# First W1 chunk loaded ahead of the values, first keys ahead of the first queries, and a new set of ranks, in a sparse-attention and feed-forward kernel

## The chip, the cores and the metric

The kernel runs on one core of a Trainium2 chip. The metric is device time in microseconds of one execution; the number to predict is the median of such executions. The core has a matrix engine (TensorE, PE in the profile; its weight loads are PEld), a vector engine (VectorE, DVE), a scalar engine (ScalarE, ACT), GpSimd (POOL) and a queue engine (SyncE, SP) that here only issues DMAs. Each engine works through its own list of instructions in order and waits at semaphores for the others.

## What is computed

```python
def reference(q, k, v, sampled_blocks, g_ln, w_ch1, w_ch2):      # B=4, H=8, S=768, D=64
    scores = q @ k^T / sqrt(64)
    # 24 blocks of 32: neighbours, the first and last block, and 3 sampled blocks per row
    scores = where(mask, scores, -1e9)
    attn = softmax(scores) ; x = (attn @ v) as [4, 768, 512]
    xn = (x - mean(x)) / sqrt(var(x) + 1e-6) * g_ln
    return x + relu(xn @ w_ch1) @ w_ch2                             # 512 -> 2048 -> 512
```

The two weight matrices come as 64-bit floats (4 bytes of each element's 8 cannot be used directly), so the kernel rebuilds 32-bit numbers from the bits on the chip and splits each into a high and a low 16-bit half.

## The kernel before, in words

**Tiling.** The 4 x 768 queries are cut into 12 units of 256 (`units`). A unit has four segments (`segs`, 48 in all), one for each pair of heads, and a segment has four slots: a slot is one head and 128 queries against all 768 keys. For a segment, TensorE forms scores in two groups (`scores`, L602, 12 matmuls a group, the two heads of 128 queries; the first segment uses 32-bit operands). VectorE adds the mask and takes the row maximum (`masked_max`, L611), ScalarE exponentiates (`exponent`, L625). In the first nine segments (`EARLY`) TensorE then transposes the probabilities (L640), ScalarE copies them out of the accumulators (L647) and TensorE multiplies by the values (L728); the later segments transpose by DMA. After four segments a unit is normalised (`layer_norm`: L809, L827, L838, L863, L877) and goes through the two products of the feed-forward part (`ffn`, both at L313, operands `w1h`, `w1l`, then `w2h`, `w2l`).

**Weights.** W1 is handled in 8 chunks (1 MB each), W2 in 16 (512 KB each). `loads_w` issues the load of a chunk (L508, L518), VectorE shifts and masks the bits in two or three operations (L529, L533, then L537, or L542 with an addition on GpSimd at L547), ScalarE scales and forms the high half (L565, L571, L573; a few by DMA at L583), and the low half is a subtraction on VectorE or GpSimd (L579, L577). The keys and queries are split in a like manner (L363, L370, L395, L400). Which engine does which step of which chunk stands in the tables `PORC`, `HIDMA`, `LOWDVE`, `KDVE`, `QDVE`, `CASTQ`, `XDVE`.

**Order.** Nothing is ordered by hand. Each step is a task of a `Plan` with an engine, a cost, what it comes after, and a rank. `Plan.run` goes through planned time and, on each engine, takes among the tasks that can start soonest the one of lowest rank; the instructions are emitted in that order. The rank of a step of attention is about its slot's number; the loads and splits of keys, values and queries are placed by `KAT`, `VAT`, `QAT`, the chunks of W1 and W2 by the tables `W1AT` and `W2AT`, with the load itself at `rank - LEAD`. Where the plan sees TensorE idle it puts in matmuls on constants into a free accumulator (`filler`, L305), which compute nothing that is used.

**Loads.** All loads named here are issued by SP, in the plan's order. The program gives the DMAs of the SP and ACT queues eight completion semaphores in turn, so from the ninth on each issue first waits for the load eight places before it.

In the kernel before, the first chunk's load is a task that comes after the first keys and the first queries:

```python
        if i == 0:
            lw.after += [kt[0, 0].raw, qt[0].raw]
```

Of the kernel before, what the change touches and what calls it, by code (L numbers as in the profile page):

```python
# [176 lines left out]
def sparse_attention_moe(  # L177
# [14 lines left out]
    B, NPAIR, NCH, _, CH = qs.shape  # L192
# [13 lines left out]
    UPS = H * TS  # L206

    EARLY = 9
    EARLYLN = 1
    EASY, EASE = 34, (232, 2529, 1055)  # L210
    PORC = ((2, 0), (2, 7), (1, 1), (2, 13), (2, 10), (1, 4), (2, 1), (1, 0))
    XACT = 4
    XDVE = 0
    RAWS_S = 1
    SPLITAT = 13.44
    VDVE = 1
    KDVE, QDVE = 12, 5
    HIDMA = ((1, 1), (1, 6), (2, 5), (2, 3), (2, 12), (2, 6), (2, 2), (2, 4))
    LEAD = -4.15
    POOLQ = ()  # L220
    WIDEAT = 16
    HIGHAT, LOWAT = -3.61, 0.01
    EVAC, EXPO = -23.3, 2.93
    PLAIN = 'full'
    LOWDVE = ((2, 2), (1, 1), (2, 11), (1, 7), (2, 4), (2, 6), (2, 3), (1, 0), (2, 9), (2, 13), (1, 6), (1, 2))
    AVHOLD = 4
    KEEP = 90000.0
    CASTK, CASTQ = 16, 5
    MASKAT = 11.99
    KAT, VAT, QAT = 4.32, 10.55, 11.84  # L230
    AVAT = -18.16
    W1AT = (5.59, 9.73, 14.79, 15.09, 18.96, 21.75, 22.98, 26.73)
    W2AT = (4.96, 6.46, 7.35, 7.59, 7.79, 8.12, 8.15, 8.19, 8.29, 8.43, 8.78, 8.9, 10.5, 10.66, 10.72, 13.23)

# [20 lines left out]
    plan = Plan()  # L255
# [226 lines left out]
    def loads_w(kind, i, before, w1done, low_tail):  # L482

        o = SimpleNamespace()
        own = (kind, i)
# [64 lines left out]
        if kind == 2 and i >= 10:  # L550
            after += tuple(low_tail)
        ld = plan.add(*queue_of(qw)[1:], load, after if kind == 1 or i >= 10 else after + tuple(
            w1done if not low_tail and i > 1 else ()), rank - LEAD, 2000,
            load=2900 * size, take=take, order="w")
        o.load = ld
# [438 lines left out]
    for b in range(B):  # L994
        for pr in range(NPAIR):
            order.append(((UPS * NCH * b) + 4 * pr - (8 if b else KAT), 0, b, pr))
            order.append(((UPS * NCH * b) + 4 * pr + VAT, 2, b, pr))
# [157 lines left out]
```

## Time and profile before

| | |
|---|---|
| time, median of 3 runs | 792.12 us (791.73 to 793.36) |
| span of the profiled execution (first to last instruction) | 790.0 us |
| PE busy in that span | 778.1 us, 98% |
| DVE, ACT, POOL busy | 621.5, 509.4, 105.2 us |

The profile's own time is its span; 2.1 us of the median lie outside it (792.12 less 790.0). In the profile a busy PE is a PE with at least one matmul under way; matmuls are pipelined, so busy time overlaps and a short wait can hide inside it.

### The profile page before, as it was taken

What the parts mean: (1) busy time and instruction counts of PE and PEld (TensorE: products, weight loads), DVE (VectorE), ACT (ScalarE), POOL (GpSimd) and SP (SyncE); (2) the same over time, 40 slices, a digit from 0 to 9 for tenths busy, and PEclk for the clock granted to TensorE, in tenths of its full rate; (3) what the DMA queues carried; (4) which work ended last, traced back from release to release, by engine and by line L of the source; (5) the groups of instructions that cost most, each with busy time, mean ns of one, the idle gap of its engine ahead of it and who ended that gap; (6) DMA issues with size and microseconds to landing.
All of it is one profiled execution on the core that took longest, in us unless ns stands there. A gap on an engine that the chain in (4) does not pass through costs nothing.

```text
span 790.0 us, 18464 instructions
## 1 busy us (share of the span) xinstructions
PE 778.1 (98%) x7336; PEld 600.0 (76%) x7336; DVE 621.5 (79%) x1225; ACT 509.4 (64%) x948; POOL 105.2 (13%) x117
## 2 busy tenths in 40 slices
PE   8999999999999999999999999999999999999998
PEld 5655677778777777777777777777777777788887
DVE  6989999988988788989878878888877878854220
ACT  6888876687666667777766766667656657652110
POOL 0444332200101000001011012021000100000000
PEclk9999999999999999999999999999999999999999
DMA  9553545978977688998785787887766656561000
GB/s 324 181 147 109 161 135 153 231 161 164 165 134 129 139 128 162 169 192 157 144 135 124 132 163 132 172 166 156 137 131 112 140 118 110 121 122 25 21 1 27
DMA packets 285638, 109.27 MB, mean 138 GB/s; under 512 B 253808, under 2 KB 277360, under 8 KB 285552
## 3 DMA queue, kind: packets, MB, share of 16 engines
q1 hardware_dynamic: 278544, 104.91, 61.1%
q0 software_dynamic: 6720, 3.08, 3.5%
q8 instruction: 57, 0.93, 0.5%
q14 instruction: 29, 0.24, 0.1%
q10 hardware_dynamic: 288, 0.10, 0.1%
HBM read 42.97 MB, written 6.29 MB: 62 GB/s over the span
## 4 chain that ended last, share of the span: by engine, by line
PE 89%; DVE 6%; ACT 2%; DMA 1%; issue 1%; SPq 1%; POOL 0%; ACTq 0%
PE bank L313 65%; PE ps L602 11%; PE pa L732 7%; PE pa L737 3%; PE pa L728 1%; DVE p L611 1%; DMA w1r<-w 1%; PE bank L640 1%; DVE w2h L533 1%; ACT pt L647 1%; DVE w2h L529 0%; DVE allow L328 0%; DVE w2h L537 0%; ACT p L625 0%; POOL w2h L547 0%
## 5 line engine op out<-in xcount | busy, mean ns | idle before, releaser
L313 PE MATMUL bank<-hh,w2h 128*128 128x256 f16 x768 | 204.5, 273 | 0.0
L313 PE MATMUL bank<-hh,w2l 128*128 128x256 f16 x768 | 204.1, 273 | 0.0
L313 PE MATMUL bank<-hl,w2h 128*128 128x256 f16 x768 | 204.1, 273 | 0.0
L611 DVE CUSTOM_DVE_ANT_1 p<-ps,allow 128x768 f32<-128x768 f32 x184 | 170.1, 951 | 24.0 <-PE ps L602 23.8
L625 ACT ACTIVATE p<-p,st 128x768 f32<-128x768 f32 x184 | 170.5, 928 | 15.7 <-DVE st L611 15.5
L313 PEld LDWEIGHTS <-w2h 128*128 128x128 f16 x1536 | 147.4, 98 | 25.8 <-issue 8.9
L313 PEld LDWEIGHTS <-w1h 128*128 128x128 f16 x1536 | 148.7, 98 | 23.6 <-issue 6.7
L313 PE MATMUL bank<-xh,w1h 128*128 128x256 f16 x768 | 115.4, 273 | 1.4 <-ACT pt L647 1.4
L313 PE MATMUL bank<-xh,w1l 128*128 128x256 f16 x768 | 115.4, 273 | 0.0
L313 PE MATMUL bank<-xl,w1h 128*128 128x256 f16 x768 | 115.3, 273 | 0.0
L916 DVE SCALAR_TENSOR_TENSOR hl<-bank,hh 128x512 f16<-128x512 f32 x96 | 66.2, 689 | 48.5 <-ACT hh L910 47.7
L910 ACT ACTIVATE hh<-bank 128x512 f16<-128x512 f32 x96 | 57.0, 594 | 65.4 <-PE bank L313 64.7
L688 ACT ACTIVATE ph<-p,st 128x768 f16<-128x768 f32 x92 | 83.5, 927 | 19.6 <-issue 8.2
L692 DVE SCALAR_TENSOR_TENSOR pl<-p,st,ph 128x768 f16<-128x768 f32 x92 | 94.3, 1042 | 1.2 <-DMA pt<-pl 1.0
L313 PEld LDWEIGHTS <-w1l 128*128 128x128 f16 x768 | 73.3, 98 | 13.7 <-issue 5.5
L313 PEld LDWEIGHTS <-w2l 128*128 128x128 f16 x768 | 75.0, 98 | 8.9 <-issue 0.2
L732 PE MATMUL pa<-pt,vh 128*64 128x512 f16 x468 | 79.2, 383 | 0.0
L688 ACT ACTIVATE raw<-p,st 128x768 f16<-128x768 f32 x64 | 57.9, 928 | 25.6 <-issue 14.7
L397 POOL DMA_DIRECT2D qh<-q x43 | 24.6, 571 | 333.7 <-PE ps L602 299.7
L692 DVE SCALAR_TENSOR_TENSOR raw<-p,st,raw 128x768 f16<-128x768 f32 x64 | 67.0, 1062 | 0.0
L602 PE MATMUL ps<-kh,qh 64*128 64x512 f16 (+1 forms) x376 | 64.9, 328 | 0.6 <-DVE st L611 0.5
L737 PE MATMUL pa<-pt,vl 128*64 128x256 f16 x468 | 64.6, 273 | 0.0
(125 smaller groups left out, 986.7 us busy)
## 6 DMA issues: line engine op xcount, KB each, us to landing
qr<-q SPq DMA_DIRECT2D x48, 128.0 KB, 3.0
raw<-k SPq DMA_DIRECT2D x16, 384.0 KB, 3.9
vr<-v SPq DMA_DIRECT2D x32, 192.0 KB, 2.9
out<-ot SPq DMA_DIRECT2D x48, 128.0 KB, 1.9
raw<-w SPq DMA_DIRECT2D x11, 512.0 KB, 3.8
w2l<-w SPq DMA_DIRECT2D x4, 1024.0 KB, 8.0
qh<-q POOLq DMA_DIRECT2D x43, 64.0 KB, 3.0
w1r<-w SPq DMA_DIRECT2D x2, 1024.0 KB, 8.3
```

The lines of the kernel that those rows point to most:

```text
L313: nc.tensor.matmul(dst, w, x, start=start, stop=stop, skip_group_check=True)
L397: o.high = plan.add("POOL", 560, lambda: nc.gpsimd.dma_start(o.qh, qs[u.b, pr, u.c]), (o.raw,), rank, 2300, load=600, order="q")
L533: nc.vector.scalar_tensor_tensor(out=o.wf, in0=o.raw[:, :, 1], scalar=-0x40000000, in1=o.wf, op0=ALU.bitwise_and, op1=ALU.bitwise_or)
L602: nc.tensor.matmul(s.ps[:, lo:hi], x[rows, s.qs], y[rows, lo:hi], start=n == 0, stop=n == len(terms) - 1)
L611: nc.vector.tensor_tensor_reduce(out=s.p.rearrange(blk, k=BLK), in0=s.ps[:, 0:S].rearrange(blk, k=BLK), in1=bias, scale=-0.125, scalar=3.0 ...
L625: nc.scalar.activation(s.p, s.p, AF.Exp, bias=s.st[:, j : j + 1], scale=-1.0, accum_out=total)
L688: nc.scalar.activation(s.ph, s.p, AF.Copy, scale=s.r)
L692: nc.vector.scalar_tensor_tensor(out=s.pl, in0=s.p, scalar=s.r, in1=s.ph, op0=ALU.mult, op1=ALU.subtract)
L732: nc.tensor.matmul(seg.pa[half[hh], 0 : 2 * CH], vo.vh[:, hh, t, :], pts[keys[hh]][:, t].rearrange("p i n -> p (i n)"), start=t == 0, stop ...
L737: nc.tensor.matmul(seg.pa[half[hh], 0:CH], vo.vl[:, hh, t, :], pts[keys[hh]][:, t, 0, :], start=False, stop=t == KT - 1, skip_group_check= ...
L910: nc.scalar.activation(u.hh[:, f : f + 2, :].rearrange("p f n -> p (f n)"), bank[plan.where("bank", own)], AF.Relu)
L916: nc.vector.scalar_tensor_tensor(out=u.hl[:, f : f + 2, :].rearrange("p f n -> p (f n)"), in0=bank[plan.where("bank", own)], scalar=0.0, i ...
```

## The change

The load of W1's first chunk no longer comes after the first keys and queries, and gets a rank of its own (`W1LEAD`); the first keys get one, too (`KFIRST`). All other numbers of placement are new, some steps change engines, and 61 tasks get a number added to their rank by a new table (`NUDGE`).

```diff
-    EASY, EASE = 34, (232, 2529, 1055)
-    PORC = ((2, 0), (2, 7), (1, 1), (2, 13), (2, 10), (1, 4), (2, 1), (1, 0))
+    EASY, EASE = 36, (232, 2529, 1055)
+    PORC = ((1, 1), (1, 5), (2, 0), (2, 1), (2, 3), (2, 5), (2, 7), (2, 10))
-    XDVE = 0
+    XDVE = 2
-    KDVE, QDVE = 12, 5
+    KDVE, QDVE = 8, 10
+    W1LEAD = -1.21
+    KFIRST = -12.57
-    LOWDVE = ((2, 2), (1, 1), (2, 11), (1, 7), (2, 4), (2, 6), (2, 3), (1, 0), (2, 9), (2, 13), (1, 6), (1, 2))
+    LOWDVE = ((1, 1), (1, 6), (1, 7), (2, 0), (2, 3), (2, 4), (2, 5), (2, 6), (2, 7), (2, 9), (2, 10), (2, 13), (2, 15))
-    CASTK, CASTQ = 16, 5
+    CASTK, CASTQ = 16, 7
-    MASKAT = 11.99
-    KAT, VAT, QAT = 4.32, 10.55, 11.84
+    MASKAT = 32.06
+    KAT, VAT, QAT = 8.91, 8.01, 3.36
+    NUDGE = {
+        1: 88.6, 31: -99.5, 41: 65.7, 46: -97.0, 273: 113.4, 282: 0.9, 288: -223.4, 296: 18.5,
...
         ld = plan.add(*queue_of(qw)[1:], load, after if kind == 1 or i >= 10 else after + tuple(
-            w1done if not low_tail and i > 1 else ()), rank - LEAD, 2000,
-            load=2900 * size, take=take, order="w")
+            w1done if not low_tail and i > 1 else ()), W1LEAD if own == (1, 0) else rank - LEAD,
+            2000, load=2900 * size, take=take, order="w")
...
-            order.append(((UPS * NCH * b) + 4 * pr - (8 if b else KAT), 0, b, pr))
+            order.append((KFIRST if (b, pr) == (0, 0) else (UPS * NCH * b) + 4 * pr - (8 if b else KAT), 0, b, pr))
...
-        if i == 0:
-            lw.after += [kt[0, 0].raw, qt[0].raw]
-            for x in lw.after[-2:]:
-                x.next.append(lw)
-                lw.left += 1
...
+    for n, by in NUDGE.items():
+        plan.tasks[n].rank += by
     plan.run()
```

What it does to the queues is seen at three places. Line numbers of the changed kernel are 13 higher there. First, the start of SP's queue; `raw` are keys, `qr` queries, `vh` and `vl` the first values, `w1r0`, `w1r1` and the first `w2l` the stages of W1's chunks 0, 1 and 2. Before:

```order
L388 DMA qr0_131<-q 128x256
L388 DMA qr1_133<-q 128x256
L360 DMA raw0_115<-k 128x768
L388 DMA qr2_139<-q 128x256
L360 DMA raw1_116<-k 128x768
L1015 DMA g_sb_113<-g 128x4x1
L470 DMA vh0_149<-v 128x384
L470 DMA vl0_150<-v 128x384
L470 DMA vh1_155<-v 128x384
L508 DMA w1r0_189<-w1 128x4x512
L508 DMA w1r1_193<-w1 128x4x512
```

and in the changed kernel:

```order
L373 DMA raw0_115<-k 128x768
L373 DMA raw1_116<-k 128x768
L401 DMA qr0_137<-q 128x256
L521 DMA w1r0_139<-w1 128x4x512
L401 DMA qr1_141<-q 128x256
L521 DMA w1r1_144<-w1 128x4x512
L521 DMA w2l_130<-w1 128x4x512
L401 DMA qr2_158<-q 128x256
L483 DMA vh0_189<-v 128x384
L483 DMA vl0_190<-v 128x384
```

Chunk 0 moves from the tenth issue to the fourth, chunks 1 and 2 come ahead of the first values as well, and the first queries move from first to third.

Second, VectorE's queue from the first pair of maxima on (each maximum is a row of `p` at L611 or L624, with a row of its accumulator `st` behind it). Before:

```order
L611 ISA p0_121,st0_201<-ps0_183,allow_109 128x768
L611 ISA st0_201 128x1
L363 TENSOR_TENSOR kl1_143<-raw1_116,kh1_142 128x768
L611 ISA p1_122,st0_201<-ps1_184,allow_109 128x768
L611 ISA st0_201 128x1
L529 TENSOR_SCALAR w2h_129<-w1r0_189 128x1024
L611 ISA p2_123,st2_255<-ps2_240,allow_109 128x768
L611 ISA st2_255 128x1
L611 ISA p3_124,st2_255<-ps3_241,allow_109 128x768
L611 ISA st2_255 128x1
L533 SCALAR_TENSOR_TENSOR w2h_129<-w1r0_189,w2h_129 128x1024
```

and in the changed kernel:

```order
L624 ISA p1_122,st0_197<-ps1_184,allow_109 128x768
L624 ISA st0_197 128x1
L542 TENSOR_SCALAR w2h_129<-w1r0_139 128x1024
L413 TENSOR_TENSOR ql0_117<-qr1_141,qh1_142 128x256
L546 SCALAR_TENSOR_TENSOR w2h_129<-w1r0_139,w2h_129 128x1024
L624 ISA p2_123,st2_238<-ps2_222,allow_109 128x768
L624 ISA st2_238 128x1
L550 SCALAR_TENSOR_TENSOR w2h_129<-w1r0_139,w2h_129 128x1024
L660 COPY pt0_0_244<-bank2_100 128x2x128
L624 ISA p3_124,st2_238<-ps3_223,allow_109 128x768
```

The three steps on chunk 0 now stand between the second and the fourth maximum, and a copy of transposed probabilities, ScalarE's work before, is among them.

Third, VectorE's queue where the second part of the mask is built (`allow`, L325 to L330 before). Before, it stands ahead of the ninth and tenth maximum:

```order
L542 TENSOR_SCALAR w1r1_193<-w1r1_193 128x1024
L325 TENSOR_TENSOR w1h_127<-allow_109,samp_i_110 128x288
L328 TENSOR_TENSOR allow_109<-allow_109,w1h_127 128x96 x3
L330 TENSOR_SCALAR allow_109<-allow_109 128x96
L760 TENSOR_TENSOR xT0_372<-pa0_373,xT0_372 128x256
L611 ISA p2_123,st8_435<-ps8_416,allow_109 128x768
```

and in the changed kernel behind them:

```order
L624 ISA p3_124,st8_448<-ps9_428,allow_109 128x768
L624 ISA st8_448 128x1
L413 TENSOR_TENSOR ql2_119<-qr3_251,qh3_252 128x256
L338 TENSOR_TENSOR w1h_127<-allow_109,samp_i_110 128x288
L341 TENSOR_TENSOR allow_109<-allow_109,w1h_127 128x96 x3
L343 TENSOR_SCALAR allow_109<-allow_109 128x96
L624 ISA ph_125,st10_494<-ps10_473,allow_109 128x768
```

The mask's second part moves behind the fifth pair of maxima, and steps on chunks 0 to 2 of W1 take its place.

## Rows read from the trace of the kernel before

**Rows 1.** Windows: stretch, its length, busy us by engine (count), clock, DMA share, GB/s

```profile
0.00:20.00 20.00, 17.40 (x124) 11.88 (x125) 13.13 (x31) 12.48 (x24) 1.27 (x7) 1.00 0.92 325
20.00:60.00 40.00, 36.57 (x321) 24.03 (x321) 37.36 (x65) 33.76 (x73) 17.73 (x13) 1.00 0.56 168
60.00:100.00 40.00, 37.59 (x320) 25.24 (x320) 38.87 (x71) 35.34 (x80) 13.86 (x13) 1.00 0.43 135
100.00:700.00 600.00, 600.00 (x5779) 463.06 (x5774) 505.57 (x1013) 410.29 (x742) 72.29 (x86) 1.00 0.74 147
700.00:790.00 90.00, 86.55 (x801) 75.75 (x799) 26.61 (x49) 17.54 (x33) 0.00 (x0) 1.00 0.14 30
```

**Rows 2.** Waits of PE: who waited for whom, us in total, times, longest

```profile
PE bank L640 <- ACT pt L647: 3.4, 6, 1.1
PE bank L313 <- ACT pt L647: 1.4, 1, 1.4
```

**Rows 3.** Groups by form: shapes, count, busy us, mean ns, idle before

```profile
L305 PE MATMUL bank<-ones,ones_h 128*128 128x256 f16 x84 | 11.9, 298 | 1.2 <-DVE eps L280 1.2
```

**Rows 4.** Chain that ended last: start us, us, what, in the head

```profile
44.01 1.08 PE ps L602 x12
45.68 2.74 PE pa L728 x24
...
74.61 1.08 PE ps L602 x12
...
102.89 7.86 PE bank L313 x72
110.75 1.08 PE ps L602 x12
```

**Rows 5.** Timeline, first 13 us: start, us, engine, line, instruction, idle before it

```profile
0.74 0.89 SPq L388 DMA_DIRECT2D qr<-q  x2
...
1.69 0.43 SPq L360 DMA_DIRECT2D raw<-k  x1
...
5.13 1.28 SPq L508 DMA_DIRECT2D w1r<-w  x2
...
6.04 0.83 ACT L370 CAST kh<-raw 128x768 f16<-128x768 f32 x1 [1.78 <-DMA raw<-k]
...
6.15 1.56 PE L602 MATMUL ps<-raw,qr 64*128 64x512 f32 x8 [1.20 <-DMA raw<-k]
...
9.86 0.95 DVE L611 CUSTOM_DVE_ANT_1 p<-ps,allow 128x768 f32<-128x768 f32 x1
...
12.52 0.70 DVE L529 TENSOR_SCALAR w2h<-w1r 128x1024 int32<-128x1024 int32 x1 [1.71 <-DMA w1r<-w]
```

**Rows 6.** DMA rate in GB/s, one number per us from 0 to 40

```profile
GB/s 0 24 252 239 360 341 163 311 389 404 412 397 395 386 396 412 411 413 414 388 404 395 405 401 407 413 331 84 116 166 23 253 24 54 0 8 0 0 0 0
```

**Rows 7.** Timeline of DVE from 17 us: the next row's start ends a step

```profile
17.77 0.95 DVE L611 CUSTOM_DVE_ANT_1 pl<-ps,allow 128x768 f32<-128x768 f32 x1
...
18.65 0.69 DVE L542 TENSOR_SCALAR w1r<-w1r 128x1024 int32<-128x1024 int32 x1
19.25 1.22 DVE L533 SCALAR_TENSOR_TENSOR w2h<-w1r,w2h 128x1024 int32<-128x1024 int32 x1
20.39 0.95 DVE L611 CUSTOM_DVE_ANT_1 p<-ps,allow 128x768 f32<-128x768 f32 x1
...
24.11 0.44 DVE L325 TENSOR_TENSOR w1h<-allow,samp_i 128x288 f32<-128x288 f32 x1
24.58 2.93 DVE L328 TENSOR_TENSOR allow<-allow,w1h 128x96 f32<-128x96 f32 x3
```

**Rows 8.** Timeline of all engines: PE transposes, then POOL and DVE side by side

```profile
16.09 1.77 PE L640 MATMUL bank<-ident,p 128*128 128x128 f32 x12
...
55.85 4.24 POOL L577 TENSOR_TENSOR w1l<-w2h,w1h 128x1024 f16<-128x1024 f32 x2
...
58.41 1.71 DVE L1063 TENSOR_SCALAR nm<-nm 128x4 f32<-128x4 f32 x1 [0.91 <-ACT p L625]
```

More of the change, by code (lines that the diff above doesn't have):

```diff
@@ L209, in sparse_attention_moe @@
     EARLYLN = 1
-    EASY, EASE = 34, (232, 2529, 1055)
-    PORC = ((2, 0), (2, 7), (1, 1), (2, 13), (2, 10), (1, 4), (2, 1), (1, 0))
+    EASY, EASE = 36, (232, 2529, 1055)
+    PORC = ((1, 1), (1, 5), (2, 0), (2, 1), (2, 3), (2, 5), (2, 7), (2, 10))
     XACT = 4
-    XDVE = 0
+    XDVE = 2
     RAWS_S = 1
-    SPLITAT = 13.44
+    SPLITAT = 0.67
     VDVE = 1
-    KDVE, QDVE = 12, 5
-    HIDMA = ((1, 1), (1, 6), (2, 5), (2, 3), (2, 12), (2, 6), (2, 2), (2, 4))
-    LEAD = -4.15
+    KDVE, QDVE = 8, 10
+    HIDMA = ((1, 1), (1, 2), (1, 5), (2, 4), (2, 7), (2, 9), (2, 12), (2, 15))
+    LEAD = -1.99
+    W1LEAD = -1.21
+    KFIRST = -12.57
     POOLQ = ()
-    WIDEAT = 16
-    HIGHAT, LOWAT = -3.61, 0.01
-    EVAC, EXPO = -23.3, 2.93
+    WIDEAT = 23
+    HIGHAT, LOWAT = 2.9, -5.81
+    EVAC, EXPO = -22.76, 12.61
     PLAIN = 'full'
-    LOWDVE = ((2, 2), (1, 1), (2, 11), (1, 7), (2, 4), (2, 6), (2, 3), (1, 0), (2, 9), (2, 13), (1, 6), (1, 2))
+    LOWDVE = ((1, 1), (1, 6), (1, 7), (2, 0), (2, 3), (2, 4), (2, 5), (2, 6), (2, 7), (2, 9), (2, 10), (2, 13), (2, 15))
     AVHOLD = 4
     KEEP = 90000.0
-    CASTK, CASTQ = 16, 5
-    MASKAT = 11.99
-    KAT, VAT, QAT = 4.32, 10.55, 11.84
-    AVAT = -18.16
-    W1AT = (5.59, 9.73, 14.79, 15.09, 18.96, 21.75, 22.98, 26.73)
-    W2AT = (4.96, 6.46, 7.35, 7.59, 7.79, 8.12, 8.15, 8.19, 8.29, 8.43, 8.78, 8.9, 10.5, 10.66, 10.72, 13.23)
+    CASTK, CASTQ = 16, 7
+    MASKAT = 32.06
+    KAT, VAT, QAT = 8.91, 8.01, 3.36
+    AVAT = -22.91
+    W1AT = (-18.23, 1.52, 4.62, 6.71, 17.65, 23.09, 29.38, 31.74)
+    W2AT = (-59.17, -56.65, -41.56, -38.84, -31.54, -30.19, -30.13, -27.57, -25.65, -24.42, -22.28, -20.76, -12.67, -11.13, -6.19, -3.13)
+    NUDGE = {
[9 rows of a table added]
+    }
     const = ctx.enter_context(tc.tile_pool(name="const", bufs=1))
```

8 rows, old and new, of the table NUDGE are left out of this document.

## The prediction

> **What bounds the kernel now.** I read the windows first. From 100 to 700 us the matrix engine is busy all the time, and after 700 us it misses only the last few us, in which results are stored [rows 1]. The change takes away no matmul but filler, and after the first unit the same work follows on PE in a similar order, so those 690 us go on as they are. Only the first 100 us have room: PE is busy 91.6 of them (17.40, 36.57 and 37.59), while VectorE is busy 37.36 of 40 and 38.87 of 40 us, and ScalarE 33.76 and 35.34 [rows 1]. So the head is bound by VectorE, with ScalarE close behind. PE's seen waits there are mostly for ScalarE's copies of transposed probabilities [rows 2]; besides, 84 filler matmuls are run [rows 3].
>
> To add up what the head loses, filler included, I take PE's useful work up to a landmark from the times at which the next row starts: a score group 1.08 us, a transpose 0.136 (12 in 1.77 less the tail), an early value group 2.64 up to its successor, a feed-forward matmul 0.109 (72 in 7.86) [rows 4, 8]; for the rest I estimate 1.45 us for a 32-bit score group, 0.54 for a spread and 0.48 for a mean's matmul. **Lost time** is a landmark's time less the useful work ahead of it:
>
> - ninth score group: 44.0 - 27.3 = 16.7 us;
> - fourteenth: 74.6 - 53.0 = 21.6 us;
> - nineteenth: 110.75 - 87.9 = 22.9 us [rows 4], and from there PE loses nothing more.
>
> The changed kernel's time is 792.12 us plus the change of that 22.9. Its 790.0 us span and the 2.1 us around it move alike.
>
> **The change part by part. The first loads.** Before, queries are issued at 0.74 and the first keys at 1.69 us, chunk 0 of W1 at 5.13 [rows 5]. Keys reach ScalarE at 6.04 and the chunk reaches VectorE at 12.52, which ends a wait of 1.71 us [rows 5]. The rates [rows 6] sum to the bytes issued up to and with the keys (0.66 MB plus part of 0.1 MB of mask) at 4.6 us and up to and with the chunk (2.92 MB) at 11.1: in both, data is used 1.4 us after its bytes are through. In the new order the keys have 0.45 MB, the first queries 1.02 MB and the chunk 2.07 MB up to their end. By the same rates that is 3.7, 5.4 and 9.0 us, so with 1.4 added 5.1, 6.8 and 10.4. If big loads in flight earlier fill the slow first microseconds, all are up to 1.7 us sooner; I take the rates as seen. So keys come 0.9 us sooner, but the first scores start at 6.9 instead of 6.15, because queries are now third. Both key subtractions are then done ahead of the first maximum. That one starts at 8.6 (6.9 + 1.56 + 0.2), the second at 9.5 instead of 9.86, and VectorE is free at 10.4, just as the chunk arrives. The 1.71 us wait is gone.
>
> What the load is moved past: the first values now stand behind 3 MB of W1. They are there by 17.3 us (4.8 MB by the rates, plus 1.4) and wanted at about 22, so this costs nothing; if that cover were gone, the first value group would wait for the difference. SP itself waits longer (an issue waits for the load eight places earlier, and the fourth keys for the second score pair), but some 5 MB are in flight by then.
>
> **VectorE's queue from there.** Steps cost, start to start: a maximum or key subtraction 0.88, the three steps of a W1 chunk 0.60, 1.14 and 1.14 (0.60 with GpSimd's addition), the second mask part 3.6 (24.11 to the end of its last step) [rows 7]; a query subtraction is 0.34 and a W1 low half 1.21 by my estimate from these. Summing the queues, VectorE has 5.6 us of work up to the second maximum before and 4.9 after, and is free of its wait at 12.5 and 10.4: a head start of (12.5 - 5.6) - (10.4 - 4.9) = 1.4 us. Against it stands what is put in early, up to the maxima of pair
>
> - 3: 11.8 us of work before, 14.1 after;
> - 8: 35.4 and 39.3;
> - 10: 46.0 and 48.7;
> - 12: 57.6 and 56.1;
> - 13: 60.9 and 62.4;
>
> and up to the first unit's `xl` (L877) 72.9 and 71.8. So up to pair 10 the new order is later by 1 to 2.5 us (W1 steps ahead of maxima, two copies, five more query subtractions of 0.34). From pair 12 on it is ahead, because the W1 work is then behind it and two low halves have left VectorE for GpSimd. ScalarE shows the same: up to the 24th exponential it has 2.4 us less to do than before (the centred squares and seven copies come later), though two query casts and two scalings are added for good, one high half less.
>
> **Walked down by hand**, holding each maximum until its scores are there and each score group until the maxima two slots back are done: the ninth score group starts at 45.6 with 27.85 us of PE work ahead of it, lost 17.7 (before 16.7). The eleventh is at 55.1, lost 18.1, as before. At the fourteenth PE itself is the last to be ready: 71.4 - 53.0 = 18.4 (before 21.6). The fifteenth waits 0.6 us for its maxima, the sixteenth 0.5 us for exponential 29 and its copy, which stand behind ScalarE's part of the normalisation. That makes 19.5. The walk has no small waits on banks and copies. Before, those that are seen are 4.8 us [rows 2], most of them in a ScalarE that was full; with ScalarE ahead I keep a quarter, 1.2 us. **Lost time after: 20.7 us, a gain of 22.9 - 20.7 = 2.2 us: 789.9.** The bounds are the walk with VectorE never idle after 10.4 (lost 17.4, gain 5.5: 786.6) and all 4.8 us of small waits as before (lost 24.3, loss 1.4: 793.5).
>
> The filler shrinks from 84 to 70 matmuls. It only fills waits, so no gain is booked for it; were one of them in the way, it costs 0.12 us. The clock stays at its upper level, 2.4 GHz, through all of the head (1.00) [rows 1], with PE waits of up to 1.4 us in it [rows 2], so I book no change.
>
> **The rivals. ScalarE hides it.** If ScalarE is the true limit from the ninth group on, its extra work (two casts of about 0.35, two scalings less one high half of about 1.0, less two copies of 0.28) costs some 1.1 us and eats VectorE's head start: lost 21.5 to 23, a time of 790.7 to 792.2, no change. For it: 35.34 of 40 us busy [rows 1] and the waits for its copies [rows 2]. Against it: the 24th exponential has less work ahead.
>
> **GpSimd holds VectorE.** At 55.85 GpSimd runs two low halves in 4.24 us, up to 60.09. A tiny VectorE step that starts at 58.41 lasts 1.71 us, to 60.12 [rows 8]. So such a pair of steps can run one after the other. In the change five W1 low halves are GpSimd's instead of three. At 1.5 us each the two more cost 3.0 us of VectorE, less what five query subtractions and one addition no longer block there: lost 22.5 to 23.7, 791.7 to 792.9, no change. Against it: GpSimd's work in the head shrinks by some 3 us in sum. The Trainium skill's page "SBUF — State Buffer", section "Who interferes with whom", has this as an exclusive lock: the one that starts second is blocked until the first has ended. These rows agree, to 0.03 us; by it, moving low halves to GpSimd speaks against this change.
>
> **Slower: the early W1 steps delay the softmax for good.** Place: VectorE between the second and the eighteenth maximum, where the walk has the new order 1.0 us behind at the ninth group, and up to 1.4 at the eighth. Small waits that meet it there (an exponential behind the chunk's scaling and high half on ScalarE, then its transposes) are not won back if PE finds no other work. With 1.0 to 1.4 us lost and the later saving absent, lost is 24 to 25 and the time 793.2 to 794.3. It decides when the fourteenth group comes later than 75.5 us. For it: the ninth to eleventh groups have no feed-forward work beside them. Against it: the mask's 3.6 us, which stand ahead of pair 5 before, now stand behind it.
>
> That the change does not do what it says is excluded by the queues: chunk 0 is the fourth load.
>
> **How the numbers follow.** About 0.2%, 1.6 us, is what a measurement of this kernel can tell from no change. The forecast, a gain of over 1.6 us: 0.54. ScalarE hides it: 0.22; GpSimd holds VectorE: 0.11; slower by over 1.6: 0.13. The first is faster, the next two are the same, the last is slower. The range runs from the lower bound, 786.6, to 793.4, the near end of the slower case; left out are some 0.1 on each side.
>
> **What would show it.** Right: chunk 0's first step on VectorE at 9 to 10.5 us with no wait for the load, the first scores at 6.2 to 6.9, the ninth score group later than 45 us, the fourteenth near 71 to 72.5, PE without waits from about 100 us, and 700 us of PE after that unchanged. Wrong: waits of PE on copies at L660 that add to more than 4.8 us, VectorE steps of 1.5 us and more beside GpSimd's low halves, a first value group that waits for its load, or a clock under 1.00 in the head.

## The result, and the profile after

The changed kernel takes 798.32 us (median of 4 runs, 795.63 to 798.76), the kernel before 791.92 in the same session: a ratio of 1.0071 (95% interval 1.0058 to 1.0084). It is slower, by some 6 us (5.6 by the ratio, 6.4 by the medians); the forecast was 789.9, and the range, 786.6 to 793.4, does not hold the time. The profiled execution has a span of 796.9 us, against 790.0.

Windows of the changed kernel, columns as in [rows 1]:

```profile
0.00:20.00 20.00, 17.53 (x115) 11.40 (x117) 14.32 (x31) 12.37 (x21) 3.12 (x7) 1.00 0.94 343
20.00:60.00 40.00, 36.68 (x318) 23.33 (x316) 37.45 (x73) 36.11 (x79) 14.28 (x9) 1.00 0.58 185
60.00:100.00 40.00, 34.49 (x284) 22.83 (x281) 34.14 (x63) 30.30 (x71) 11.61 (x11) 0.91 0.37 102
100.00:700.00 600.00, 598.30 (x5751) 462.21 (x5749) 499.71 (x1010) 410.48 (x742) 77.71 (x89) 1.00 0.74 146
```

Against [rows 1] the first 60 us are as good as before. From 60 to 100 us TensorE is busy 34.49 us instead of 37.59, VectorE 34.14 instead of 38.87, and the clock is 0.91 instead of 1.00: every engine does less in the same time there. From 100 to 700 us TensorE misses 1.7 us; before, it missed nothing.

The same window cut finer. First two slices of the kernel before, then three of the changed one:

```profile
64.00:68.00 4.00, 4.00 (x36) 2.50 (x32) 4.00 (x6) 3.79 (x8) 0.44 (x1) 1.00 0.08 14
68.00:72.00 4.00, 3.49 (x26) 1.85 (x25) 4.00 (x8) 4.00 (x10) 4.00 (x2) 1.00 0.00 0
```

```profile
64.00:68.00 4.00, 0.70 (x2) 0.30 (x2) 4.00 (x4) 1.05 (x2) 1.83 (x1) 0.70 0.13 16
68.00:72.00 4.00, 3.69 (x19) 2.05 (x20) 2.87 (x7) 3.85 (x11) 0.00 (x0) 0.50 0.02 4
72.00:76.00 4.00, 4.00 (x32) 2.68 (x34) 3.96 (x8) 3.04 (x7) 0.00 (x0) 0.95 0.00 0
```

TensorE's waits, in the form of [rows 2], show a new longest one of 3.6 us for the copies of transposed probabilities, and three that are later, in the stage of the feed-forward products:

```profile
PE bank L653 <- ACT pt L660: 6.7, 7, 3.6
...
PE bank L326 <- DVE hl L929: 0.8, 1, 0.8
PE pa L745 <- ACT hh L923: 0.6, 1, 0.6
...
PE pa L745 <- DMA pt<-pl: 0.2, 1, 0.2
```

The timeline at the first of these places (start, us, engine, line, instruction, idle before it) tells the whole first loss:

```profile
56.52 0.57 POOL L410 DMA_DIRECT2D qh<-q  x1
...
62.10 0.43 DVE L413 TENSOR_TENSOR ql<-qr,qh 128x256 f16<-128x256 f32 x1 [1.99 <-DMA qh<-q]
...
62.44 1.22 DVE L546 SCALAR_TENSOR_TENSOR w2h<-w2l,w2h 128x1024 int32<-128x1024 int32 x1
...
63.71 2.12 POOL L590 TENSOR_TENSOR w1l<-w2h,w1h 128x1024 f16<-128x1024 f32 x1 [0.36 <-DMA w1h<-w2h]
63.91 3.00 DVE L550 SCALAR_TENSOR_TENSOR w2h<-w2l,w2h 128x1024 int32<-128x1024 int32 x1
...
66.94 1.06 ACT L586 ACTIVATE w1h<-w2h 128x1024 f16<-128x1024 f32 x1 [4.73 <-DVE w2h L550]
...
68.31 1.54 PE L653 MATMUL bank<-ident,p 128*128 128x128 f32 x6 [3.57 <-ACT pt L660]
```

GpSimd issues the cast of query 8's high half (`qh`) at 56.52, behind an addition for chunk 5 (L560) that starts at 54.18. VectorE's next step in order is that query's low half (`ql`), and it waits 1.99 us for the cast. The query itself is not wanted before the 17th score group, at 95.9 us. Behind the subtraction stand the steps on W1's chunk 6. The third of them (L550) takes 3.00 us instead of the 1.14 of [rows 7]: it ends 1.08 us after GpSimd's low half, that is, it did not run beside it. ScalarE's next step in order is that chunk's high half (L586), so it waits 4.73 us; the copies of transposed probabilities (L660) that would have been ready to run stand behind it, and TensorE, whose accumulators wait to be copied out, stops for 3.57 us. Then it works on at the lower of its two clock levels, 1.2 GHz (granted 0.50): six transposes take 1.54 us, and 0.82 in a run below in which the clock stays up.

By the reckoning of the prediction (a landmark's time less the useful work ahead of it; here the start of the group's first matmul, and for a late value group an estimate of 2.15 us), the lost time at five score groups is:

| score group | 12 | 14 | 19 | 23 | 27 |
|---|---|---|---|---|---|
| before | 18.1 | 21.5 | 22.8 | 23.3 | 23.7 |
| changed | 18.9 | 25.7 | 26.8 | 27.4 | 30.5 |

Two places carry the loss: 6.8 us from the 12th to the 14th group (before 3.4), and 3.1 from the 23rd to the 27th (before 0.4). After that both kernels run alike. (The spans differ by 6.9 us, the lost times by 6.8. The kernel before has no wait of TensorE behind the 19th group; the 0.9 us that its row still grows is the error of the estimates.) The chain that ended last names both places, with a piece each that is a transfer:

```profile
56.52 5.55 DMA qh<-q
...
169.13 4.62 DMA pt<-pl
```

### The profile page after: what moved, and what is told of

Same layout as the page of the kernel before. It is cut to its first block, busy times and chain, and to the rows that moved or that the text cites. A ratio compares the mean times of both kernels' runs of the same rounds, so it can differ in the third digit from the quotient of the medians.

```text
span 796.9 us, 18430 instructions
## 1 busy us (share of the span) xinstructions
PE 780.5 (98%) x7322; PEld 601.1 (75%) x7322; DVE 616.2 (77%) x1229; ACT 510.5 (64%) x948; POOL 106.7 (13%) x115
## 4 chain that ended last, share of the span: by engine, by line
PE 83%; DVE 8%; DMA 3%; issue 3%; ACT 2%; POOL 1%; ACTq 0%; DVEq 0%; POOLq 0%
PE bank L326 59%; PE ps L615 11%; PE pa L745 7%; PE pa L750 3%; DMA qh<-q 1%; PE bank L653 1%; DVE pl L705 1%; DMA pt<-pl 1%; PE pa L741 1%; DVE p L624 1%; ACT pt L660 1%; DMA allow<-blocks 1%; DVE xc L876 1%; DVE raw L546 1%; DVE w2h L550 1%
## 5 line engine op out<-in xcount | busy, mean ns | idle before, releaser
L624 DVE CUSTOM_DVE_ANT_1 p<-ps,allow 128x768 f32<-128x768 f32 x183 | 169.2, 951 | 28.1 <-PE ps L615 27.7
L701 ACT ACTIVATE ph<-p,st 128x768 f16<-128x768 f32 x106 | 95.8, 928 | 38.0 <-DVE st L692 22.4
L705 DVE SCALAR_TENSOR_TENSOR pl<-p,st,ph 128x768 f16<-128x768 f32 x106 | 106.2, 1016 | 2.8 <-DMA pt<-pl 2.5
L745 PE MATMUL pa<-pt,vh 128*64 128x512 f16 x468 | 79.9, 383 | 0.8 <-ACT hh L923 0.6
L750 PE MATMUL pa<-pt,vl 128*64 128x256 f16 x468 | 65.5, 273 | 0.0
L615 PE MATMUL ps<-kl,qh 64*128 64x512 f16 (+1 forms) x376 | 63.3, 325 | 0.0
L615 PEld LDWEIGHTS <-qh 64*128 64x128 f16 x752 | 30.1, 94 | 43.6 <-issue 21.9
```

The source lines that it names most:

```text
L615: nc.tensor.matmul(s.ps[:, lo:hi], x[rows, s.qs], y[rows, lo:hi], start=n == 0, stop=n == len(terms) - 1)
L624: nc.vector.tensor_tensor_reduce(out=s.p.rearrange(blk, k=BLK), in0=s.ps[:, 0:S].rearrange(blk, k=BLK), in1=bias, scale=-0.125, scalar=3.0 ...
L701: nc.scalar.activation(s.ph, s.p, AF.Copy, scale=s.r)
L705: nc.vector.scalar_tensor_tensor(out=s.pl, in0=s.p, scalar=s.r, in1=s.ph, op0=ALU.mult, op1=ALU.subtract)
L745: nc.tensor.matmul(seg.pa[half[hh], 0 : 2 * CH], vo.vh[:, hh, t, :], pts[keys[hh]][:, t].rearrange("p i n -> p (i n)"), start=t == 0, stop ...
L750: nc.tensor.matmul(seg.pa[half[hh], 0:CH], vo.vl[:, hh, t, :], pts[keys[hh]][:, t, 0, :], start=False, stop=t == KT - 1, skip_group_check= ...
```

## The experiments

Except where an instruction is added or left out, the experiments compute the plan of their parent kernel and then emit single steps at another place in it; no other instruction changes its place on any engine. The diffs show the queue of the engine that changes. Each time is given with the ratio to the kernel before in the same session.

**Is it query 8's subtraction?** First, that one step is moved on VectorE:

```diff
 L542 TENSOR_SCALAR w2h<-w2l 128x1024
-L413 TENSOR_TENSOR ql<-qr,qh 128x256
 L546 SCALAR_TENSOR_TENSOR w2h<-w2l,w2h 128x1024
...
 L624 ISA pl,st<-ps,allow 128x768
 L624 ISA st 128x1
+L413 TENSOR_TENSOR ql<-qr,qh 128x256
 L592 SCALAR_TENSOR_TENSOR w1l<-w2h,w1h 128x4x256
```

> The changed kernel with one VectorE step moved: the low half of query 8 (`ql<-qr,qh`, L413), which waited 1.99 us at 62.10 us for its cast, stands seven steps later, behind the maxima of the twelfth score group; nothing else moves on any engine. Theory Q (VectorE is held in order by that wait, GpSimd's low half then falls on the next W1 step, ScalarE and its copies wait behind that step, and TensorE stops for 3.57 us and falls to half its clock): VectorE reaches the third step of W1's chunk 6 at about 61.9 instead of 63.9 us, ahead of GpSimd's low half at 63.7, so that step takes 1.1 instead of 3.0 us; the 13th score group comes at 65.5 to 67 instead of 69.8 us, the clock stays at 1.00, and the time falls from 798.3 by 3.5 to 5 us, to 793.3 to 794.8, or further, to about 791, if the 2.3 us that are lost between 156 and 176 us come from the same delay. Theory W (the W1 steps that the change puts early make VectorE late whatever waits there): VectorE has no room, the wait returns at another step, and the time stays above 796.8.

Measured: 791.78 us, 0.9999 (0.9988 to 1.0010). One subtraction of 0.43 us, moved by seven steps, gives back all that the change had cost. That is more than theory Q had priced (793.3 to 794.8), and not for the reason it gave for a time near 791: the second loss stays. The 13th group comes at 64.6 (expected 65.5 to 67), the 14th at 73.0 us, the clock is 1.00. Timeline of that kernel:

```profile
59.72 1.23 DVE L546 SCALAR_TENSOR_TENSOR w2h<-w2l,w2h 128x1024 int32<-128x1024 int32 x1
61.20 1.22 DVE L550 SCALAR_TENSOR_TENSOR w2h<-w2l,w2h 128x1024 int32<-128x1024 int32 x1
...
62.44 1.06 ACT L586 ACTIVATE w1h<-w2h 128x1024 f16<-128x1024 f32 x1 [0.69 <-DVE w2h L550]
...
63.22 2.13 POOL L590 TENSOR_TENSOR w1l<-w2h,w1h 128x1024 f16<-128x1024 f32 x1 [0.33 <-DMA w1h<-w2h]
64.08 1.55 DVE L413 TENSOR_TENSOR ql<-qr,qh 128x256 f16<-128x256 f32 x1
```

Chunk 6 is through VectorE before GpSimd's low half starts. Now the subtraction is held beside GpSimd (1.55 us), and nobody waits for it. The lost time is 18.5, 20.0, 20.7, 21.4 and 24.6 us at the five groups: the first loss is gone, the second (3.2) is not. At the 19th group this kernel is 2.1 us ahead of the kernel before, and that pays for most of the second loss.

The step can stay where it is if the cast comes sooner. On GpSimd:

```diff
 L590 TENSOR_TENSOR w1l<-w2h,w1h 128x4x256
-L560 TENSOR_TENSOR w2h<-w2h,w2l 128x1024
 L410 DMA qh<-q 128x256
+L560 TENSOR_TENSOR w2h<-w2h,w2l 128x1024
 L590 TENSOR_TENSOR w1l<-w2h,w1h 128x4x256
```

> The changed kernel with one step moved on GpSimd: it issues query 8's cast (L410) ahead of its addition for chunk 5 of W1 (L560) instead of behind it. VectorE's queue is as in the changed kernel, with query 8's subtraction where it was. Theory Q: the cast is issued near 51 instead of 56.5 us, while hardly any other transfer is under way (0 to 18 GB/s at 50 to 54 us), lands some 3 us later, VectorE does not wait at that subtraction, and the time is that of the run in which the subtraction itself is moved, to 0.5 us: 793.3 to 794.8, or about 791. A rival, that it is the step's place and its 0.4 us on VectorE and not the late cast: the time stays within 0.5 us of 798.3 here, and only moving the step helps. Theory W: above 796.8.

Measured: 792.38 us, 1.0008 (0.9998 to 1.0019); 18.5 us lost at the 12th and 19.9 at the 14th group, as in the first run. So it is the late cast, not the step. Two details of the expectation missed: the cast was issued at 52.98, not near 51, and landed 7 us later, not 3, with the loads of the last W1 chunk and of two W2 chunks, 2 MB, issued beside it at 52.4 to 53.8; VectorE still waits 0.47 us for it, and 1.5 us sooner was enough.

**Is it the early load itself?** In the changed kernel, the three W1 loads go back behind queries and first values:

```diff
 L401 DMA qr<-q 128x256
-L521 DMA w1r<-w 128x4x512
 L401 DMA qr<-q 128x256
-L521 DMA w1r<-w 128x4x512
-L521 DMA w2l<-w 128x4x512
 L401 DMA qr<-q 128x256
 L483 DMA vh<-v 128x384
 L483 DMA vl<-v 128x384
+L521 DMA w1r<-w 128x4x512
+L521 DMA w1r<-w 128x4x512
+L521 DMA w2l<-w 128x4x512
```

> The changed kernel with its headline part undone on SyncE's queue alone: the loads of W1's chunks 0, 1 and 2 are issued behind the first three queries and the first values, as before the change; all other queues are as in the changed kernel. Theory W (the early loads of W1 are what costs): the time falls by most of the 6.4 us, to 792 to 794.5. Theory Q (they cost nothing by themselves): VectorE waits some 2 us for chunk 0 at 10 us again, since its steps stand ahead of the third maximum; the later landmarks come up to 2 us later, and the time is 798 to 800.5.

Measured: 799.90 us, 1.0095 (1.0071 to 1.0118), slower still. VectorE's wait for the chunk is back, and the 12th group has lost 20.1 us instead of 18.9:

```profile
11.99 0.69 DVE L542 TENSOR_SCALAR w2h<-w1r 128x1024 int32<-128x1024 int32 x1 [1.66 <-DMA w1r<-w]
```

In the kernel before, the headline part alone was tried twice. The first time, SyncE's queue got the changed kernel's start:

```diff
+L360 DMA raw<-k 128x768
+L360 DMA raw<-k 128x768
 L388 DMA qr<-q 128x256
+L508 DMA w1r<-w 128x4x512
 L388 DMA qr<-q 128x256
-L360 DMA raw<-k 128x768
 L388 DMA qr<-q 128x256
-L360 DMA raw<-k 128x768
...
-L508 DMA w1r<-w 128x4x512
```

> The kernel before with only the headline part of the change, on SyncE's queue alone: first keys, second keys, first queries, chunk 0 of W1, and then the rest in its old order; every other queue is as in the kernel before. Theory Q (the early load is harmless): VectorE's wait of 1.71 us for chunk 0 at 12.5 us is gone or under 0.5 us, the ninth score group comes 0 to 1.7 us sooner than 44.0, and the time is 790.4 to 792.1. Theory W (the early load itself costs): slower than 793.5.

Measured: 798.59 us, 1.0081 (1.0063 to 1.0099). By the words on record this speaks for theory W. The trace says otherwise:

```profile
9.80 0.40 ACT L395 CAST qh<-qr 128x256 f16<-128x256 f32 x1 [6.84 <-DMA qr<-q]
...
10.23 0.43 DVE L400 TENSOR_TENSOR ql<-qr,qh 128x256 f16<-128x256 f32 x1 [9.08 <-ACT qh L395]
...
12.95 0.95 DVE L611 CUSTOM_DVE_ANT_1 p<-ps,allow 128x768 f32<-128x768 f32 x1
```

In the old queues query 1's cast is ScalarE's first step and its subtraction VectorE's first; its load, moved behind the chunk, held both engines, and the first maximum came at 12.95 instead of 9.86 [rows 5]. It is the same mechanism at another place, and my edit had made it. The second time the chunk alone moved, behind all loads that the first steps need:

```diff
 L360 DMA raw<-k 128x768
+L508 DMA w1r<-w 128x4x512
 L1015 DMA g_sb<-g 128x4x1
...
 L470 DMA vh<-v 128x384
-L508 DMA w1r<-w 128x4x512
```

> The kernel before with the load of W1's chunk 0 alone moved on SyncE's queue: directly behind the second keys, the last of the loads that the first steps of VectorE and ScalarE work on (queries 1 and 2 and keys 1 stay ahead of it; in the run with a reordered start they came behind the chunk, and ScalarE waited 6.84 and VectorE 9.08 us for query 1). Theory P (an early chunk costs nothing where nothing that is needed sooner stands behind it): the chunk's bytes end at 2.2 instead of 2.9 MB, VectorE's wait of 1.71 us for it shrinks below 0.6 us, the ninth score group comes 0 to 1.5 us sooner than 44.0 us, the time is 789.8 to 791.5. Theory W (any early W1 load costs): 793 or more.

Measured: 791.28 us, 0.9995 (0.9986 to 1.0004). The chunk's first step starts at 10.26, without a wait, instead of 12.52 after one of 1.71 [rows 5]. VectorE then waits 1.22 us for the next scores, so of the 2.3 us it keeps 0.5 at the 12th group. The early load alone costs nothing; a gain of that size the times do not tell from none, since the interval holds 1.

**How the first loss is made up.** TensorE's gap was filled with 29 matmuls that compute nothing that is used (`paf` is an accumulator that stands idle then):

```diff
 L822 MATMUL bank<-xT,ones 128x256
+L318 LDWEIGHTS ones_h
+L318 MATMUL paf<-ones,ones_h 128x256
...
```

> The changed kernel, all queues as they are, with 29 filler matmuls more on TensorE, between the mean's matmul at 64.05 us and the transposes that waited 3.57 us; they write an accumulator (`pa`) that nobody uses then, and at 0.117 us each fill 3.4 us of that gap. Theory C (part of the 6.4 us is the clock: it was granted at 0.50 from 66 us and the work behind the gap ran at half speed): the clock stays at 1.00 through 64 to 76 us, the transposes at 68.3 take 0.8 instead of 1.5 us and the 13th score group 1.1 instead of 2.0 us, the 14th group comes 1 to 1.7 us sooner than 78.7, and the time falls to 796.6 to 797.3. Theory N (VectorE and ScalarE are what is late, and TensorE's clock costs nothing there): the time stays within 0.5 us of 798.3.

Measured: 796.68 us, 1.0063 (1.0046 to 1.0081): by the times alone not to be told from the changed kernel. And the profiled execution, at 795.13 the fastest of four, had one more difference:

```profile
63.84 1.21 DVE L550 SCALAR_TENSOR_TENSOR w2h<-w2l,w2h 128x1024 int32<-128x1024 int32 x1
...
64.06 2.99 POOL L590 TENSOR_TENSOR w1l<-w2h,w1h 128x1024 f16<-128x1024 f32 x1 [0.70 <-DMA w1h<-w2h]
```

Here GpSimd's input landed later, VectorE's step started first, took 1.21 us, and GpSimd's took 2.99. So it mixes the two, and a third: with VectorE's step not held the gap is shorter than the filler, which runs to 67.84 us and so holds up the transposes itself (they start at 67.68; in the next run, without filler, at 66.43). The next runs part them. GpSimd's low half of chunk 5 is left out:

```diff
 L410 DMA qh<-q 128x256
-L590 TENSOR_TENSOR w1l<-w2h,w1h 128x4x256
 L410 DMA qh<-q 128x256
```

> The changed kernel without GpSimd's low half of W1's chunk 5 (L590, 2.12 us from 63.71 us on); that part of `w1l` is set to zero at the start, so this leaves out one low half of the weights. VectorE still waits 1.99 us for query 8's cast. Theory L (GpSimd's step keeps VectorE's third step on chunk 6 from running, 3.00 us instead of 1.14): that step ends near 65.05 instead of 66.91, ScalarE's wait of 4.73 us and TensorE's of 3.57 us shrink by 1.9 us, and the time falls by 1.9 to 3 us, to 795.3 to 796.4; the wait for the cast then carries the other 3 to 4 us. Theory M (the step is long for another reason, or the wait for the cast carries all): it still takes over 2 us, or the time stays above 797.5.

Measured: 795.14 us, 1.0037 (1.0023 to 1.0051). L550 takes 1.21 us, TensorE waits 1.78 us instead of 3.57. Then the same work as two instructions:

```diff
-L590 TENSOR_TENSOR w1l<-w2h,w1h 128x4x256
+L590 TENSOR_TENSOR w1l<-w2h,w1h 128x256
+L590 TENSOR_TENSOR w1l<-w2h,w1h 128x3x256
```

> The changed kernel with GpSimd's low half of W1's chunk 5 as two instructions, a quarter of it first (about 0.6 us from 63.7 us on) and three quarters then; the same numbers are computed and nothing else moves. In the changed kernel this step started at 63.71 and VectorE's step at 63.91, which then lasted 3.00 us; in the run with the filler GpSimd's started at 64.06, VectorE's at 63.84, and VectorE's took 1.21 and GpSimd's 2.99 us. Theory L (of the two engines the one that starts second is held until the other's instruction has ended, so 0.2 us decide over 1.9): VectorE's step is held only by the first piece, ends near 65.4 instead of 66.9 us, GpSimd's second piece is the one held, and the time falls to 795 to 796.8, as without the step (795.1). Theory G (GpSimd keeps its hold from one instruction to the next): VectorE's step still takes about 3 us and the time stays at 798 to 799.

Measured: 795.36 us, 1.0051 (1.0038 to 1.0064), with one instruction more and nothing left out: 3.0 us under the changed kernel by the medians, 1.6 by the ratios, whose intervals overlap. Its timeline (both pieces of GpSimd's step in one row):

```profile
62.88 3.26 POOL L590 TENSOR_TENSOR w1l<-w2h,w1h 128x256 f16<-128x256 f32 x2
63.09 1.56 DVE L550 SCALAR_TENSOR_TENSOR w2h<-w2l,w2h 128x1024 int32<-128x1024 int32 x1
```

VectorE's step is held by the first quarter only, and then GpSimd's second piece by VectorE. Into this kernel's remaining gap of 2.12 us went 17 filler matmuls:

```diff
 L822 MATMUL bank<-xT,ones 128x256
+L318 LDWEIGHTS ones_h
+L318 MATMUL paf<-ones,ones_h 128x256
...
```

> The kernel with GpSimd's low half in two instructions (795.36, in which VectorE's step is not held for 1.9 us and TensorE's wait for the copies is 2.12 us), with 17 filler matmuls more in that wait (0.117 us each, 2.0 us) into the idle accumulator; nothing else moves. In the run with 29 fillers the profiled execution had VectorE's step unheld too, so clock and hold were mixed there; here both kernels have it unheld. Theory C (the lower clock, granted 0.76 and 0.81 in 64 to 72 us, costs TensorE 1 to 1.4 us): the clock stays at 1.00, the 14th score group comes 1 to 1.4 us sooner than 76.2, and the time falls to 794.0 to 794.4. Theory N (the clock costs nothing, VectorE and ScalarE are late anyway): the 14th group stays within 0.4 us of 76.2 and the time within 0.5 us of 795.4.

Measured: 794.59 us, 1.0035 (1.0021 to 1.0049), 0.8 us less, which the two intervals alone do not part; the profiled executions do. The 14th group comes at 75.35, 0.85 us sooner than 76.20, which lies between the two theories; but in this execution the cast landed later and the 12th group was already 0.5 us behind, so from there it gains 1.4. Windows of the kernel without the filler:

```profile
64.00:68.00 4.00, 1.95 (x10) 1.35 (x12) 4.00 (x8) 3.31 (x7) 2.15 (x1) 0.76 0.03 5
68.00:72.00 4.00, 4.00 (x32) 2.02 (x28) 2.84 (x9) 3.35 (x9) 0.00 (x0) 0.81 0.00 0
```

And with it:

```profile
64.00:68.00 4.00, 3.74 (x29) 2.80 (x31) 4.00 (x6) 2.56 (x6) 2.92 (x2) 1.00 0.15 20
68.00:72.00 4.00, 4.00 (x40) 2.44 (x34) 3.97 (x11) 4.00 (x10) 0.00 (x0) 1.00 0.00 0
```

With TensorE busy the clock stays at its upper level. Lost between the 12th and the 14th group: 6.8 us in the changed kernel, 4.8 with the low half in two pieces (2.0 less), 3.4 with the gap filled as well (1.4 less), 1.5 with the subtraction moved (1.9 less, the length of the wait). So of the 5.3 us that query 8's subtraction costs in this stretch, the wait itself is 1.9, GpSimd's hold 2.0 and the clock 1.4. This split is rough: it takes one profiled execution of each kernel and takes the causes away in this order. In the kernel with the two pieces the cast also landed a little sooner (VectorE waited 1.67 us for it, not 1.99), and the clock fell less (0.81 instead of 0.50 from 68 to 72 us), so the 2.0 hold some of both.

**The second loss.** The timeline of the changed kernel there:

```profile
162.79 0.95 DVE L376 TENSOR_TENSOR kl<-raw,kh 128x768 f16<-128x768 f32 x1
...
163.66 0.95 DVE L624 CUSTOM_DVE_ANT_1 p<-ps,allow 128x768 f32<-128x768 f32 x1
...
164.87 0.68 DVE L929 SCALAR_TENSOR_TENSOR hl<-bank,hh 128x512 f16<-128x512 f32 x1
...
165.61 0.60 PE L326 MATMUL bank<-xh,w1h 128*128 128x256 f16 x4 [0.83 <-DVE hl L929]
165.80 1.94 DVE L705 SCALAR_TENSOR_TENSOR pl<-p,st,ph 128x768 f16<-128x768 f32 x2
...
167.82 2.55 SPq L714 DMA_TRANSPOSE pt<-pl  x2
...
173.26 0.38 PE L745 MATMUL pa<-pt,vh 128*64 128x512 f16 x1 [0.64 <-ACT hh L923]
```

VectorE has no idle time from 161 to 171.8 us, and TensorE waits for two of its results: the hidden layer's low half `hl`, and the transposes of `pl` for a value group (L745; the row names ScalarE's `hh`, which it does not read, and the row behind it says `pt<-pl`). In front of both stand low halves of values and keys (L450, L376); keys 5 are first read at the 27th group, at 190.8 us. First `hl` alone was put forward, on top of the moved subtraction:

```diff
+L929 SCALAR_TENSOR_TENSOR hl<-bank,hh 128x512
 L624 ISA p,st<-ps,allow 128x768
 L624 ISA st 128x1
 L945 SCALAR_TENSOR_TENSOR ot_2<-bank,xT 128x256
-L929 SCALAR_TENSOR_TENSOR hl<-bank,hh 128x512
```

> The kernel in which query 8's subtraction stands behind the maxima (791.8), with one more move on VectorE: the first low half of the second unit's hidden layer (`hl`, L929), for which TensorE waited 0.79 us at 158.7 us, is put ahead of the second maximum of the 23rd score group and one result step (L945) instead of behind them. Theory H (in the stage from 150 to 180 us TensorE loses to VectorE's order, step by step): that wait of 0.79 us is gone and the time falls by 0.8 us, to 791.0, while the loss at the 25th group, which is put down to the transposes of `pl`, stays. Theory F (VectorE is simply full there, and its whole load is what costs): the wait comes back at another step and the time stays within 0.3 us of 791.8.

Measured: 792.53 us, 1.0005 (0.9996 to 1.0014), no gain. The wait for `hl` is gone, TensorE waits 1.5 us for the transposes instead, and 2.4 us are still lost from the 23rd to the 27th group (2.3 and 3.2 in the two kernels of the first experiments). `hl` alone was not the bound. Then `pl` and its transposes as well, on VectorE (above) and SyncE (the last four lines, two of its four transposes):

```diff
-L450 SCALAR_TENSOR_TENSOR vl<-vr_0,vh 128x384
-L450 SCALAR_TENSOR_TENSOR vl<-vr_1,vh 128x384
-L376 TENSOR_TENSOR kl<-raw,kh 128x768
+L705 SCALAR_TENSOR_TENSOR pl<-p,st,ph 128x768
+L705 SCALAR_TENSOR_TENSOR pl<-p,st,ph 128x768
+L929 SCALAR_TENSOR_TENSOR hl<-bank,hh 128x512
 L624 ISA p,st<-ps,allow 128x768
...
-L929 SCALAR_TENSOR_TENSOR hl<-bank,hh 128x512
 L945 SCALAR_TENSOR_TENSOR ot_3<-bank,xT 128x256
-L705 SCALAR_TENSOR_TENSOR pl<-p,st,ph 128x768
-L705 SCALAR_TENSOR_TENSOR pl<-p,st,ph 128x768
 L929 SCALAR_TENSOR_TENSOR hl<-bank,hh 128x512
+L450 SCALAR_TENSOR_TENSOR vl<-vr_0,vh 128x384
+L450 SCALAR_TENSOR_TENSOR vl<-vr_1,vh 128x384
+L376 TENSOR_TENSOR kl<-raw,kh 128x768
...
 L711 DMA_TRANSPOSE pt_1<-ph 128x6x128
+L714 DMA_TRANSPOSE pt_0<-pl 128x6x128
+L714 DMA_TRANSPOSE pt_1<-pl 128x6x128
 L951 DMA out<-ot_2 128x256
```

> The kernel in which query 8's subtraction stands behind the maxima (791.8), with VectorE's and SyncE's queues from 156 to 165 us in another order: both `pl` steps (L705) of the tenth segment and the hidden layer's first `hl` (L929) first, then the maximum and the results, and the low halves of values 3 and keys 5 and 6 behind them; on SyncE the four transposes of the tenth segment stand ahead of two stores and one load. Theory H: the waits of 0.79 us at 158.7 (for `hl`) and 0.71 us at 166.5 (for the transposed `pl`, landed at 167.2) are gone, the lost time from the 23rd to the 26th score group falls from 2.5 to under 1 us, and the time falls by 1.5 to 2.5 us, to 789.3 to 790.3, under the kernel before. Theory F (VectorE is full there): the time stays within 0.6 us of 791.8, since what is put behind is waited for next.

Measured: 790.34 us, 0.9985 (0.9976 to 0.9994): faster than the kernel before, by 1.2 us, and 7 to 8 us faster than the changed one (by the ratios, by the medians). Lost: 18.5, 19.9, 20.6, 21.2 and 21.6 us at the five groups. Its timeline at that place:

```profile
154.72 2.06 DVE L705 SCALAR_TENSOR_TENSOR pl<-p,st,ph 128x768 f16<-128x768 f32 x2
...
156.69 0.68 DVE L929 SCALAR_TENSOR_TENSOR hl<-bank,hh 128x512 f16<-128x512 f32 x1
...
158.17 2.57 SPq L714 DMA_TRANSPOSE pt<-pl  x2
```

And its window from 100 to 700 us, in which TensorE is busy all the time again:

```profile
100.00:700.00 600.00, 599.98 (x5776) 463.42 (x5774) 499.74 (x1011) 410.11 (x740) 73.38 (x87) 1.00 0.74 146
```

The same reordering without the moved subtraction:

> The changed kernel with query 8's subtraction where it was, and only the reordering of VectorE's and SyncE's queues from 156 to 165 us (both `pl` steps and the first `hl` first, low halves of values 3 and keys 5 and 6 behind, four transposes ahead of two stores and a load). Theory S (two separate losses, 5.5 us behind query 8's cast and 2 to 3 us where `pl` and its transposes are late): the lost time grows by under 0.6 us from the 23rd to the 27th score group, instead of 3.1, and the time is 795.3 to 796.8, that is 1.5 to 3 us under the changed kernel. Theory D (the second loss is only an echo of the first): with VectorE late as it is, the same waits return behind the moved steps, and the time stays above 797.5.

Measured: 796.78 us, 1.0065 (1.0052 to 1.0077). The lost time grows by 1.5 us from the 23rd to the 27th group instead of 3.1, so the second loss is no echo of the first (it stayed, too, where the first was gone), but half of it stays here: TensorE still waits 0.6 us in two pieces for `pt<-pl`. By the times alone this run is not told apart from the changed kernel.

What stays open is why the change has this second loss: it puts ten of W2's low halves on VectorE instead of seven and ranks `kl` and `vl` ahead of `pl`, but neither was undone by itself. That the order there is enough to remove it is shown, that the extra load is its cause is not.

## Why the prediction was wrong

Step by step:

- **First loads:** forecast scores at 6.9, chunk 0 on VectorE at 10.4 with no wait; seen 6.10 and 10.52, no wait. No value group waited for its load. Right, with the scores 0.8 us sooner than forecast.
- **VectorE's queue:** the ninth group forecast at 45.6 with 17.7 us lost, seen 45.74 and 17.9; the eleventh 55.1 and 18.1, seen 55.8 and 18.9. Right, a little too good.
- **The fourteenth group:** forecast 71.4, seen 78.73. Here the sum fails. The step is the one that priced the five query subtractions that move from GpSimd to VectorE at 0.34 us each. The durations were right (0.34 from start to start). Left out was what they wait for: the high halves of queries 7, 8 and 9 are made by a transfer that GpSimd issues, among the loads of W1 and W2. A row for it was there, in the waits of the kernel before:

```profile
POOL ql L400 <- DMA qh<-q: 25.5, 10, 3.4
```

The same waits in the changed kernel:

```profile
DVE ql L413 <- DMA qh<-q: 2.4, 2, 2.0
```

Before, GpSimd waited ten times for such casts, up to 3.4 us, and none of TensorE's waits [rows 2] was for GpSimd. Moving the subtractions moved two of the waits, 2.4 us in sum, to an engine in whose order the softmax stands. My walk by hand held VectorE's steps for scores and nothing else.

- **With that one step out of the way** the sum holds up to the 19th group: lost 20.7 us there, as forecast (before 22.8). That it fits to a tenth is luck: at the 14th group, at 73.0 instead of 71.4, 20.0 us are lost where the walk had 18.4, and behind it only 0.7 where the sum had 2.3. With both moves the kernel is 1.2 us faster than the one before (by the ratio); the forecast was 2.2.
- **The clock:** "no change" rested on waits of up to 1.4 us that had left it at 1.00. A stop of 3.57 us did not leave it there, and some 1.4 us were paid on top.
- **"Those 690 us go on as they are":** wrong by 2.7 us (3.1 from the 23rd to the 27th group, less the 0.4 of the kernel before). Before, VectorE was busy 37.3 of the 40 us from 140 to 180 while TensorE never waited; I took TensorE's full row for proof against a new order. What kept TensorE fed there was the old one. The kernel before there:

```profile
140.00:180.00 40.00, 40.00 (x384) 31.27 (x382) 37.29 (x71) 28.64 (x55) 6.37 (x7) 1.00 0.88 197
```

The rivals. ScalarE as the true limit (lost 21.5 to 23) does not fit the 20.7, nor the 20.6 of the kernel with both moves. GpSimd's hold was named, with the right mechanism, but priced as an average over two low halves; it was one step, some 2 us, at a place that a wait had moved into it. These runs agree with the Trainium skill's page "SBUF — State Buffer", section "Who interferes with whom", by which the order of issue decides who is blocked: 63.71 against 63.91 us held VectorE, 63.84 against 64.06 held GpSimd. The slower rival had the right landmark (the 14th group later than 75.5 us) and the wrong cause: the early W1 steps cost 0.8 us by the 12th group and were won back.

## What to carry to other kernels

When a step moves to another engine, its waits move with it: price it by what it waits for in the old engine's rows and by what stands behind it in the new engine's order, not by its duration. A step that is not due for 30 us belongs behind the steps that are due, however short it is. And a full row of the bounding engine is a statement on the order that feeds it, so a new order has to be walked through that stage too, for the results that TensorE waits for last, here a product's low half and two transposes.

## What the runs showed of the hardware

- **0.2 us decide over 1.9.** Of VectorE's third step on chunk 6 and GpSimd's low half beside it, the one that started second did nothing until the other's instruction had ended (3.00 us instead of 1.14, or 2.99 instead of 2.12). The hold goes by instruction: cut in two, GpSimd's step let VectorE in after the first quarter (1.56 us), and the kernel became 1.6 to 3 us faster (ratios, medians). Not every pair holds so: in the changed kernel a maximum that starts at 57.86, beside a low half on GpSimd from 57.11 to 59.26, takes its usual 0.95 us. That a landing time decides who starts first may be why the changed kernel's runs spread from 795.6 to 798.8; this was not tried by itself, and it can't be all, since the kernel without that GpSimd step spreads from 792.4 to 797.3.
- **A small transfer can take twice its usual time.** The 64 KB cast of a query takes 2.9 us from issue to landing in the median of 41 in the changed kernel (2.4 to 5.9). The one that mattered took 5.55, with 347 GB/s moved beside it, and the one put forward 6.93, with 312. The rate does not settle it: another took 3.39 us at 295 GB/s and another 5.69 at 169. What makes a cast late stays open.
- **A stop of TensorE costs more than its length.** After 3.57 us without work the granted clock was 0.50, the lower level, and six transposes took 1.54 us instead of 0.82. After a stop of 2.12 us it was 0.81 from 68 to 72 us; with that gap filled with matmuls that compute nothing it stayed at 1.00, and the loss up to the 14th group was 1.4 us less.
